# A planner that charges the time in which VectorE and GpSimd both work on SBUF, with three engines for one normalisation and a new table of terms

## The chip, the cores and the metric

The kernel runs on 1 core of one Trainium2 chip. The metric is the device time of one execution in microseconds, as the median of several runs. PE is TensorE, ACT ScalarE, DVE VectorE, POOL GpSimd, SP the queue that issues the DMAs.

## The reference

Three layers follow each other on 4 batches of 576 tokens and 512 features, all in fp32:

```
scores = scale * q @ k.T, within a window of 64 tokens     # 8 heads of 64
x = softmax(scores) @ v
h = relu(x @ w_in); u, v = halves of h                     # 512 -> 1024
v_n = (v - mean) / sqrt(var + 1e-6)
x = (u * (w_spatial @ v_n + b_spatial)) @ w_out
logits = x @ w_gate                                        # 4 experts, the best 2
for e in experts: ye = causal_softmax(scale*q_e @ k_e.T) @ v_e @ wo[e]
out = sum of the chosen experts' ye, weighted
```

## The kernel before

Precise products are made from two fp32r halves: a value is copied (the high half, names ending in `h`) and the copy is subtracted from it (the low half, `l`), and a product is three matmuls, as in `mm<-xh,w` and `mm<-xl,w`. So each tensor costs DVE, ACT or POOL a copy and a subtraction before PE can use it.

Phase 1 holds the first attention, the layer with `w_in` and the spatial mix; phase 2 holds the experts. In the first attention a **couple** (`a_couple`) is two groups of 192 tokens: 12 score matmuls `sc<-ut,qa` or `sc<-kt,qa`, then for each of two tiles `pa` the masked maximum on DVE (L501, three instructions each with a read of the accumulator), the exponential on ACT (L507, three), an addition and a reciprocal on DVE (L520, L522), the normalisation `s_norm` (L512, three, on POOL or DVE), three transposes on PE (L516, `at<-ident,pa`) and a copy to `pt`. Then 12 matmuls `at<-pt,v` (for the first batch `at<-pt,woh` and `at<-pt,wol`, tiles that hold `v` there) give `xh`, `xl`, which the projections `mm<-w,xh`, `mm<-xh,w` and so on read. `w_in` arrives as 64-bit words; `prep64` makes the two halves of it in six steps (L626 to L636, a copy, a subtraction). `b_mix` is the spatial mix; its first matmul is the first `mm<-wsp_h,vh`.

Nothing is issued in the order of the code. Each step is a node with its engines and their costs, and `Planner.run` walks through a modelled time: each engine takes the ready node of the lowest priority number, to which the table SHIFT adds a term for each unit of work; with several engines to choose from, a node goes where it would end first, with biases. The result is a fixed order of instructions for each engine. PE's plan also has 8 warming matmuls and 60 fillers `mm<-ident` of the lowest priority, which the plan uses where PE has nothing else. All 68 are issued, whether PE has then to wait or not.

Of the kernel before, what the change touches and what calls it, by code (L numbers as in the profile page):

```python
# [58 lines left out]


class Slot:
    def __init__(self, ring):
        self.nth, ring.asked = ring.asked, ring.asked + 1
        self.ring, self.make, self.left, self.free_at, self.t = ring, ring.make, 0, None, None

    def __getitem__(self, key):
        return self.t[key]


class Node:  # L70
    __slots__ = ("on", "emit", "prio", "wait", "next", "ready", "alloc", "use", "end", "by", "late", "form", "nth")


class Planner:
# [2 lines left out]
    ISSUE, WAY, RATE, FLIGHT = 475.0, 650.0, 360.0, 8  # L80
# [1284 lines left out]
```

## Time and profile before

| | |
|---|---|
| median of 3 runs | 464.27 us (462.72 to 464.32) |
| the profiled execution | 462.36 us, of which the span is 460.6 us |
| PE busy | 444.6 us (97%), 3962 matmuls |
| ACT, DVE, POOL busy | 289.1, 296.2, 159.7 us |
| granted TensorE clock | 0.999 of full speed |
| DMA | 32.97 MB, mean 72 GB/s |

The span runs from the first to the last instruction. PE's busy time contains the fillers and time in which matmuls overlap, so it is an upper bound of what PE has to do.

### The profile page before, as it was taken

How to read it: one execution, taken by the hardware profiler on the slowest of the kernel's cores; microseconds unless marked ns; L12 is line 12 of the kernel's file. 1: busy time of each engine (PE TensorE's matmuls, PEld its weight loads, DVE VectorE, ACT ScalarE, POOL GpSimd, SP SyncE). 2: the span in 40 equal slices, each digit the busy share in tenths (PEclk: the TensorE clock that was granted, in tenths of full speed). 3: DMA queues.
4: the chain of work that ended last, by engine and by line, in shares of the span. 5: the costliest groups of instructions: out<-in, count | busy, mean ns of one | idle time of the engine just before them, and what ended most of it. 6: DMA issues, size and time to landing. Idle time of an engine off the chain costs nothing.

```text
span 460.6 us, 10987 instructions
## 1 busy us (share of the span) xinstructions
PE 444.6 (97%) x3962; PEld 396.5 (86%) x3962; DVE 296.2 (64%) x1227; ACT 289.1 (63%) x906; POOL 159.7 (35%) x246
## 2 busy tenths in 40 slices
PE   7988998999999999999999999999999999999996
PEld 6766878997799988999899999888988988998875
DVE  3999899556583459912205346987876778858930
ACT  3867894647583337612224436898887797877953
POOL 6689587333831037700541442231031111200100
PEclk9999999999999999999999999999999999999999
DMA  8995334224242131301101000000001001000124
GB/s 268 356 308 161 124 93 156 71 78 135 65 133 61 47 91 52 89 1 54 39 1 21 26 1 2 0 2 1 1 25 46 24 2 22 25 2 1 55 85 137
DMA packets 31624, 32.97 MB, mean 72 GB/s; under 512 B 1937, under 2 KB 25489, under 8 KB 31570
## 3 DMA queue, kind: packets, MB, share of 16 engines
q1 hardware_dynamic: 31570, 32.28, 22.4%
q8 instruction: 31, 0.51, 0.4%
q14 instruction: 23, 0.19, 0.1%
HBM read 27.55 MB, written 4.72 MB: 70 GB/s over the span
## 4 chain that ended last, share of the span: by engine, by line
PE 79%; DVE 7%; DMA 4%; ACT 4%; POOL 3%; issue 1%; SPq 1%; POOLq 0%; ACTq 0%
PE mm L295 56%; PE sc L295 8%; PE at L295 8%; PE at L1180 4%; DMA y<-in_w_in_dram 3%; PE at L516 3%; ACT kd L306 1%; DVE pa L512 1%; POOL pa L512 1%; ACT p L1160 1%; SPq L384 1%; DVE wsp_l L319 1%; DVE xl L319 1%; ACT pg L306 1%; DMA qa<-in_qT_dram 1%
## 5 line engine op out<-in xcount | busy, mean ns | idle before, releaser
L295 PE MATMUL mm<-xh,w 128*128 128x288 f32 x512 | 110.3, 299 | 0.0
L295 PEld LDWEIGHTS mm<-xh,w 128*128 128x128 f32 x512 | 84.3, 188 | 1.2 <-issue 0.9
L295 PE MATMUL mm<-xl,w 128*128 128x288 f32 x256 | 75.4, 294 | 0.0
L295 PE MATMUL mm<-w,xh 128*128 128x512 f32 (+1 forms) x256 | 64.7, 342 | 0.0
L507 ACT ACTIVATE pa<-pa,mx 128x128 f32<-128x128 f32 x144 | 56.0, 395 | 9.7 <-DVE mx L501 9.5
L512 POOL TENSOR_SCALAR pa<-pa,mx 128x128 f32<-128x128 f32 x78 | 34.4, 456 | 54.5 <-ACT pa L507 29.6
L1164 POOL TENSOR_SCALAR p<-p,mc,fx 128x256 f32<-128x256 f32 (+4 forms) x24 | 16.0, 667 | 102.9 <-DVE mc L1163 48.4
L295 PEld LDWEIGHTS mm<-xl,w 128*128 128x128 f32 x256 | 48.2, 188 | 0.2
L295 PEld LDWEIGHTS mm<-w,xh 128*128 128x128 f32 x256 | 43.3, 189 | 5.0 <-issue 0.2
L1160 ACT ACTIVATE p<-p,mc 128x128 f32<-128x128 f32 (+4 forms) x72 | 41.9, 583 | 8.7 <-DVE mc L1148 4.4
L295 PE MATMUL mm<-w,xl 128*128 128x512 f32 (+1 forms) x128 | 43.2, 338 | 0.0
L295 PE MATMUL mm<-wsp_h,vh 128*128 128x288 f32 x128 | 39.0, 305 | 1.6 <-ACT ut L314 1.6
L295 PE MATMUL mm<-wsp_h,vl 128*128 128x288 f32 x128 | 37.7, 295 | 0.0
L295 PE MATMUL mm<-wsp_l,vh 128*128 128x288 f32 x128 | 37.7, 294 | 0.0
L1148 DVE CUSTOM_DVE_ANT_0 p<-sc,cmask 128x128 f32<-128x128 f32 (+4 forms) x72 | 33.7, 482 | 4.8 <-PE sc L295 3.1
L306 ACT ACTIVATE pg<-at 128x512 f32<-128x512 f32 (+4 forms) x80 | 32.3, 432 | 3.9 <-PE at L1180 3.2
L295 PE MATMUL sc<-kd,qs 128*64 128x288 f32 (+5 forms) x96 | 31.5, 342 | 0.1
L1180 PE MATMUL at<-ident,p 128*128 128x128 f32 x192 | 30.3, 276 | 1.0 <-DVE p L1164 0.3
L775 DVE TENSOR_TENSOR y<-mm,ut 128x288 f32<-128x288 f32 x24 | 10.8, 455 | 30.5 <-PE mm L295 30.5
L706 DVE BATCH_NORM_STATS2 st<-vr 128x6 f32<-128x512 f32 (+1 forms) x20 | 13.8, 690 | 25.8 <-ACT vr L314 25.4
L306 ACT ACTIVATE pt<-at 128x384 f32<-128x384 f32 x47 | 21.2, 490 | 14.0 <-PE at L516 14.0
L516 PE MATMUL at<-ident,pa 128*128 128x128 f32 x144 | 24.5, 285 | 5.7 <-DVE pa L512 3.3
(192 smaller groups left out, 1116.2 us busy)
## 6 DMA issues: line engine op xcount, KB each, us to landing
vt<-in_v_dram SPq DMA_DIRECT2D x12, 512.0 KB, 4.2
qa<-in_qT_dram SPq DMA_DIRECT2D x44, 96.0 KB, 3.2
out_dram<-ot SPq DMA_DIRECT2D x15, 256.0 KB, 2.0
y<-in_w_in_dram SPq DMA_DIRECT2D x7, 512.0 KB, 7.0
kt<-in_kT_dram SPq DMA_DIRECT2D x12, 288.0 KB, 3.1
y<-in_w_outT_dram SPq DMA_DIRECT2D x4, 512.0 KB, 3.4
y<-in_wspT_dram SPq DMA_DIRECT2D x2, 576.0 KB, 4.9
ut<-in_kT_dram SPq DMA_DIRECT2D x2, 384.0 KB, 7.5
```

The costliest lines, as they stand in the source:

```text
L295: pe.matmul(o, lhsT, rhs, start=start, stop=stop)
L306: act.activation(o, i, AF.Copy)
L319: engs[e].tensor_tensor(out=o, in0=a, in1=hi.bitcast(F32), op=ALU.subtract)
L507: act.activation(pa[:, j, :], pa[:, j, :], AF.Exp, bias=mx[:, j, 0:1], scale=-1.0, accum_out=mx[:, j, 1:2])
L512: engs[e].tensor_scalar(pa[:, j, :], pa[:, j, :], mx[:, j, 2:3], 1.0, op0=ALU.mult, op1=ALU.mult)
L516: pe.transpose(ps2[:, j * 128:(j + 1) * 128], pa[:, j, :], ident)
L706: a = N((DVE, 600), lambda e: dve.bn_stats(st[:m, 0:6], vr[:m]), [a], alloc=[st], use=[vr])
L775: dve.tensor_tensor(out=o, in0=ps[:, :HS], in1=u[:, d, tk], op=ALU.mult)
L1148: dve.tensor_tensor_reduce(out=P[:, a0:a1], in0=ps[:, :w], in1=msk, scale=-0.125, scalar=3.0e38, op0=ALU.add, op1=ALU.min, accum_out=mc[:, ...
L1160: a = N((ACT, 284 + 0.87 * L), lambda e: act.activation(P[:m, :L], P[:m, :L], AF.Exp, bias=mc[:m, 0:1], scale=-1.0, accum_out=mc[:m, 2:3]) ...
L1164: a = N({POOL: 328 + 0.832 * L, DVE: 90 + 0.52 * L}, lambda e: engs[e].tensor_scalar(P[:, :L], P[:, :L], mc[:, 3:4], fx[:, I, ev:ev + 1], ...
L1180: pe.transpose(ps[:, j * m:(j + 1) * m], P[:, j * 128:(j + 1) * 128], ident)
```

## The change

The planner's rules change in four places. A node says whether it works on SBUF alone (`sbuf=True`), and where such a node of DVE overlaps with an instruction of POOL, the plan adds the overlap to the one that starts later. A load that is issued while an earlier one is still on its way is charged 2.2 us more. The costs of switching PE between tile shapes, of score and PV groups and of matmuls change a little. And the normalisation of the first attention, `down` (the first step of `prep64`) and several copies out of PSUM may go to more engines than before. All scalars and the whole table SHIFT (3 rows of 351 terms, not shown) are replaced. The number of loads, matmuls and of all the other steps stays as it was.

```diff
-SWITCH = 58767.74293990493
+SWITCH = 227452.0
-DVE_BIAS = (1730.5970176011094, 7352.217706873879)
-POOL_BIAS = (288.01246154132895, 9897.664225472437)
+DVE_BIAS = (1146.0, 3886.0)
+POOL_BIAS = (1188.0, 5162.0)
-EFT = (772.5181606546909, 4334.303370577451)
+EFT = (534.0, 1231.0)
...
-    DRAIN = (0.0, 92.0, 91.0), (160.0, 0.0, 160.0), (75.0, 92.0, 0.0)
+    DRAIN = (0.0, 91.0, 91.0), (0.0, -78.0, 0.0), (0.0, 0.0, -78.0)
+
+    CLASH, BEHIND = 1.0, 2200.0
...
+        elif e == DVE:
+            if n.sbuf:
+                self.free[e] = n.end = n.end + self.CLASH * max(0.0, min(n.on[e], self.free[POOL] - t))
+            self.sbuf = n.sbuf
+        elif e == POOL and self.sbuf:
+            self.free[e] = n.end = n.end + self.CLASH * max(0.0, min(n.on[e], self.free[DVE] - t))
...
+                behind = self.BEHIND if self.moved[-1] > t + self.WAY else 0.0
...
-            self.free[e], n.end = t, self.moved[-1]
+            self.free[e], n.end = t, self.moved[-1] + behind
...
             def s_norm(e, pa=pa, mx=mx):
                 for j in range(3):
-                    engs[e].tensor_scalar(pa[:, j, :], pa[:, j, :], mx[:, j, 2:3], 1.0, op0=ALU.mult, op1=ALU.mult)
+                    if e == ACT:
+                        act.activation(pa[:, j, :], pa[:, j, :], AF.Copy, scale=mx[:, j, 2:3])
+                    else:
+                        engs[e].tensor_scalar(pa[:, j, :], pa[:, j, :], mx[:, j, 2:3], 1.0, op0=ALU.mult, op1=ALU.mult)
...
-            a = N({POOL: 1053, DVE: 450}, s_norm, [a], use=[pa, mx], prio=prio)
+            a = N({POOL: 1053, DVE: 450, ACT: 620}, s_norm, [a], use=[pa, mx], prio=prio, sbuf=True)
...
-        n1 = N((ACT, 520), lambda e: act.activation(a_(), word(1).bitcast(F32), AF.Copy, scale=2.0 ** -112),
-               [n0], alloc=[tmp], use=[raw], prio=prio)
...
+        n1 = N({ACT: 540, POOL: 620, DVE: 345}, down, [n0], alloc=[tmp], use=[raw], prio=prio, sbuf=True)
```

In the built program the normalisation's 144 instructions stand 78 on POOL and 66 on DVE before, and 114 on ACT, 24 on DVE and 6 on POOL in the change. POOL's rows shrink from 174 to 94.

The order moves at the start above all. First SP, the first loads, before and in the change (`ut` holds kT of the first batch, `qa` q, `woh` and `wol` v, `y` and `w` w_in):

```order
L384 DMA qa<-in_qT_dram 128x384 x2
L384 DMA y_128<-in_w_in_dram 128x1024
L384 DMA y_130<-in_w_in_dram 128x1024
L384 DMA ut<-in_kT_dram 128x2x192 x2
L384 DMA ut<-in_kT_dram 128x4x192
L384 DMA y_135<-in_w_in_dram 128x1024
```

```order
L394 DMA ut<-in_kT_dram 128x2x192 x2
L394 DMA qa<-in_qT_dram 128x384 x2
L394 DMA ut<-in_kT_dram 128x4x192
L394 DMA woh<-in_v_dram 128x2x256
L394 DMA wol<-in_v_dram 128x2x256
L394 DMA y_133<-in_w_in_dram 128x1024
```

kT is now ahead of q, and two loads of w_in that stood between q and kT come after v.

Then ACT, from its second shown instruction on, before and in the change (L507 and L517 are the exponential, L523 the normalisation, L630 and L645 `down`):

```order
L630 ACTIVATE y_140<-y_128 128x512
L630 ACTIVATE y_153<-y_130 128x512
L306 ACTIVATE w<-y_140 128x512
L507 ACTIVATE pa,mx<-pa,mx 128x128 x3
L630 ACTIVATE y_212<-y_135 128x512
L507 ACTIVATE pa,mx<-pa,mx 128x128 x3
L630 ACTIVATE w_252<-w_142 128x512
L507 ACTIVATE pa,mx<-pa,mx 128x128 x6
L306 ACTIVATE pt<-at 128x384
```

```order
L517 ACTIVATE pa,mx<-pa,mx 128x128 x6
L645 ACTIVATE y_226<-y_133 128x512
L316 ACTIVATE pt<-at 128x384
L517 ACTIVATE pa,mx<-pa,mx 128x128 x12
L523 ACTIVATE pa<-pa,mx 128x128 x3
L316 ACTIVATE w<-y_226 128x512
L316 ACTIVATE xh<-at 128x192 x2
L523 ACTIVATE pa<-pa,mx 128x128 x6
L316 ACTIVATE pt<-at 128x384 x3
```

ACT now begins with exponentials, and normalisations stand in its queue behind them.

Last PE, the rows around the last filler (`mm<-ident`) and the first projection (`mm<-w,xh`) in the change; before, the first projection stands behind five couples' scores, and 14 fillers stand behind it:

```order
L305 MATMUL mm<-ident 128x128 x7
L529 MATMUL at<-ident,pa 128x128 x3
L305 MATMUL mm<-ident 128x128 x10
L305 MATMUL sc<-ut,qa 64x128 x12
L305 MATMUL mm<-ident 128x128
L529 MATMUL at<-ident,pa 128x128 x6
L305 MATMUL sc<-kt,qa 64x128 x12
L305 MATMUL mm<-w,xh 128x512 x2
```

In the change seven couples' scores and all 68 warming matmuls and fillers stand ahead of the first projection.

## Rows read from the trace of the kernel before

**Rows 1.** Windows by stage: busy us (x instructions) of each engine.
```profile
0.00:9.81 9.81, 6.40 (x37) 6.24 (x37) 3.11 (x10) 2.67 (x4) 6.13 (x24) 1.00 0.76 248
9.81:78.15 68.34, 61.00 (x726) 50.14 (x726) 64.56 (x265) 51.40 (x188) 51.95 (x71) 1.00 0.66 211
78.15:250.00 171.85, 171.34 (x1674) 156.29 (x1675) 86.75 (x394) 82.30 (x288) 63.99 (x105) 1.00 0.21 62
250.00:450.00 200.00, 198.96 (x1495) 178.34 (x1494) 141.75 (x560) 149.17 (x422) 37.62 (x47) 1.00 0.06 20
450.00:460.60 10.60, 6.86 (x36) 5.48 (x34) 0.00 (x0) 3.62 (x7) 0.00 (x0) 0.97 0.45 148
```
Columns: stretch and its length, then busy time of PE, PEld, DVE, ACT, POOL, the granted clock, the DMA engines' busy share and GB/s.

**Rows 2.** Lines of PE from 0 to 80 us: busy us, mean ns | idle before.
```profile
L295 PE MATMUL mm<-ident 128*128 128x128 f32 x136 | 19.9, 301 | 1.6 <-DVE ident L325 1.6
```

**Rows 3.** Timeline of PE at the start: start us, length us, what [idle before <-releaser].
```profile
1.57 6.40 PE L295 MATMUL mm<-ident 128*128 128x128 f32 x36 [1.57 <-DVE ident L325]
9.81 0.89 PE L295 MATMUL sc<-ut,qa 64*64 64x128 f32 x24 [1.84 <-DMA ut<-in_kT_dram]
```

**Rows 4.** Timeline of PE where the spatial mix begins.
```profile
78.15 0.40 PE L295 MATMUL mm<-wsp_h,vh 128*128 128x288 f32 x1 [1.55 <-ACT ut L314]
```

**Rows 5.** The chain that ended last, 0 to 90 us: start us, us, what.
```profile
50.15 1.55 PE at L295 x48
...
83.72 0.66 PE at L516 x6
84.37 1.58 PE mm L295 x12
85.96 0.82 PE sc L295 x24
```

**Rows 6.** Lines of DVE from 0 to 80 us.
```profile
L501 DVE CUSTOM_DVE_ANT_0 pa<-sc,mask 128x128 f32<-128x128 f32 x54 | 12.6, 281 | 0.2 <-PE sc L295 0.2
L512 DVE TENSOR_SCALAR pa<-pa,mx 128x128 f32<-128x128 f32 x30 | 10.5, 408 | 0.1
L633 DVE SCALAR_TENSOR_TENSOR y<-y,y 128x512 int32<-128x512 int32 x10 | 8.1, 821 | 6.3 <-POOL y L626 6.2
L636 DVE SCALAR_TENSOR_TENSOR y<-y 128x512 int32<-128x512 int32 x10 | 7.7, 774 | 0.1
...
L319 DVE TENSOR_TENSOR wsp_l<-y,wsp_h 128x576 fp32r<-128x576 f32 x2 | 3.9, 1968 | 0.0
...
L628 DVE TENSOR_SCALAR y<-y 128x512 int32<-128x512 int32 x1 | 0.4, 398 | 0.0
```

**Rows 7.** Timelines of DVE and POOL, two normalisations on DVE.
```profile
13.21 2.41 DVE L512 TENSOR_SCALAR pa<-pa,mx 128x128 f32<-128x128 f32 x3
...
20.43 0.73 DVE L512 TENSOR_SCALAR pa<-pa,mx 128x128 f32<-128x128 f32 x3
21.08 0.70 DVE L636 SCALAR_TENSOR_TENSOR w<-w 128x512 int32<-128x512 int32 x1
...
13.03 1.27 POOL L319 TENSOR_TENSOR w<-y,w 128x512 fp32r<-128x512 f32 x1
14.26 0.65 POOL L626 TENSOR_SCALAR y<-y 128x512 f32<-128x512 f32 x1
```

**Rows 8.** Lines of ACT from 0 to 80 us, and its timeline at 282.8 us.
```profile
L507 ACT ACTIVATE pa<-pa,mx 128x128 f32<-128x128 f32 x60 | 23.3, 395 | 5.3 <-DVE mx L501 5.2
...
L630 ACT ACTIVATE y<-y 128x512 f32<-128x512 f32 x10 | 6.8, 678 | 7.3 <-DMA y<-in_w_in_dram 6.9 <-DVE t2w L319 0.4
...
282.80 0.91 ACT L306 ACTIVATE zt<-y 128x128 fp32r<-128x128 f32 x4
```

**Rows 9.** Windows of the first 20 us (columns as in rows 1).
```profile
0.00:10.00 10.00, 6.59 (x44) 6.43 (x48) 3.27 (x11) 2.86 (x4) 6.13 (x24) 1.00 0.77 251
10.00:20.00 10.00, 9.34 (x124) 8.01 (x120) 9.73 (x46) 8.20 (x34) 5.53 (x8) 1.00 1.05 366
```

**Rows 10.** Waits: engine line waited for: us in total, times, longest us.
```profile
ACT pa L507 <- DVE mx L501: 9.5, 10, 2.6
```

More of the change, by code (lines that the diff above doesn't have):

```diff
@@ L70 @@
 class Node:
-    __slots__ = ("on", "emit", "prio", "wait", "next", "ready", "alloc", "use", "end", "by", "late", "form", "nth")
+    __slots__ = ("on", "emit", "prio", "wait", "next", "ready", "alloc", "use", "end", "by", "late", "form", "nth", "sbuf")
 class Planner:
@@ L87, in __init__, with node @@
         self.phase = self.form = self.asked = 0
-    def node(self, on, emit, deps=(), alloc=(), use=(), prio=None, late=None, form=0):
+        self.sbuf = False
+    def node(self, on, emit, deps=(), alloc=(), use=(), prio=None, late=None, form=0, sbuf=False):
         n = Node()
-        n.form, n.nth = form, self.asked
+        n.form, n.nth, n.sbuf = form, self.asked, sbuf
         self.asked += 1
@@ L273, in t_mm @@
     def t_mm(n, m=128):
-        return max(109 if m == 128 else 53, 0.442 * n + 4.7)
+        return max(109 if m == 128 else 53, 0.4445 * n + 5.0)
     def t_act(n, psum_src=True):
@@ L545, in a_couple @@
         prio -= X_BIAS
-        o = N((PE, 760), pv, done + [PV_N.get(k[:2]) for k in grp] + vn, alloc=[ps3] + new, use=pts + hv, prio=prio,
+        o = N((PE, 848), pv, done + [PV_N.get(k[:2]) for k in grp] + vn, alloc=[ps3] + new, use=pts + hv, prio=prio,
               form=2)
@@ L554, in a_couple @@
                 cs, ss = slice(g * 192, g * 192 + w), slice(x * 192, x * 192 + w)
-                a = N((ACT, t_act(w)), lambda e, xh=xh, cs=cs, ss=ss: copy(e, xh[:, cs], ps3[:, ss]), [o], use=[ps3, xh], prio=prio)
+                a = N(on_copy(w), lambda e, xh=xh, cs=cs, ss=ss: copy(e, xh[:, cs], ps3[:, ss]), [o], use=[ps3, xh], prio=prio)
                 a = N((DVE, t_tt(w)), lambda e, xh=xh, xl=xl, cs=cs, ss=ss: sub(e, xl[:, cs], ps3[:, ss], xh[:, cs]), [a],
@@ L560, in a_couple @@
                 xt, ss = XT[b, p], slice(x * 192 + 128, x * 192 + 192)
-                a = N((ACT, 104), lambda e, xt=xt, ss=ss: copy(e, xt[:, 0, :], ps3[:, ss]), [o], use=[ps3, xt], prio=prio)
+                a = N(on_copy(64), lambda e, xt=xt, ss=ss: copy(e, xt[:, 0, :], ps3[:, ss]), [o], use=[ps3, xt], prio=prio)
                 XT_N[b, p] = N((DVE, 135), lambda e, xt=xt, ss=ss: sub(e, xt[:, 1, :], ps3[:, ss], xt[:, 0, :]), [a],
@@ L628, in sign, with down @@
                 dve.tensor_single_scalar(p_().bitcast(I32), word(1), SIGN, op=ALU.bitwise_and)
-        n1 = N((ACT, 520), lambda e: act.activation(a_(), word(1).bitcast(F32), AF.Copy, scale=2.0 ** -112),
-               [n0], alloc=[tmp], use=[raw], prio=prio)
-        n2 = N({POOL: 588, DVE: 335}, sign, [n0, n1], use=[raw, tmp], prio=prio)
+        def down(e):
+            if e == ACT:
+                act.activation(a_(), word(1).bitcast(F32), AF.Copy, scale=2.0 ** -112)
+            else:
+                engs[e].tensor_scalar(a_(), word(1).bitcast(F32), 2.0 ** -112, 1.0, op0=ALU.mult, op1=ALU.mult)
+        n1 = N({ACT: 540, POOL: 620, DVE: 345}, down, [n0], alloc=[tmp], use=[raw], prio=prio, sbuf=True)
+        n2 = N({POOL: 588, DVE: 335}, sign, [n0, n1], use=[raw, tmp], prio=prio, sbuf=True)
         n3 = N((DVE, 602), lambda e: dve.scalar_tensor_tensor(p_().bitcast(I32), word(0), 29, p_().bitcast(I32),
                                                               op0=ALU.logical_shift_right, op1=ALU.bitwise_or),
-               [n2], use=[raw, tmp], prio=prio)
+               [n2], use=[raw, tmp], prio=prio, sbuf=True)
         n4 = N((DVE, 602), lambda e: dve.scalar_tensor_tensor(a_().bitcast(I32), a_().bitcast(I32), 3, p_().bitcast(I32),
                                                               op0=ALU.logical_shift_left, op1=ALU.bitwise_or),
-               [n1, n3], use=[tmp], prio=prio)
+               [n1, n3], use=[tmp], prio=prio, sbuf=True)
         n5 = N(on_copy(512, 1, False), lambda e: copy(e, hv(), a_()), [n4, first],
-               alloc=alloc, use=[tmp] + ([] if alloc else [h]), prio=prio)
+               alloc=alloc, use=[tmp] + ([] if alloc else [h]), prio=prio, sbuf=True)
         if first is None:
             P_N[kind, k if kind == "in" else 0] = n5
-        return N({POOL: 1225, DVE: 602}, lambda e: sub(e, lv(), a_(), hv()), [n5], use=[tmp, h, l], prio=prio)
+        return N({POOL: 1225, DVE: 602}, lambda e: sub(e, lv(), a_(), hv()), [n5], use=[tmp, h, l], prio=prio, sbuf=True)
     def prep_sp(k0_, prio):
@@ L703, in b_v @@
             a = N((DVE, t_tt(512)), lambda e: dve.tensor_tensor(out=vr[:64], in0=ps[:64], in1=vr[:64], op=ALU.add), [a], use=[ps, vr])
-            a = N({ACT: 520, DVE: 335}, lambda e: relu(e, vr[:64], vr[:64]), [a], use=[vr])
+            a = N({ACT: 520, DVE: 335}, lambda e: relu(e, vr[:64], vr[:64]), [a], use=[vr], sbuf=True)
         a = N((DVE, 600), lambda e: dve.bn_stats(st[:m, 0:6], vr[:m]), [a], alloc=[st], use=[vr])
@@ L712, in b_v @@
         a = N({DVE: 460, POOL: 850}, lambda e: engs[e].tensor_scalar(
-            vr[:m], vr[:m], st[:m, 10:11], st[:m, 9:10], op0=ALU.add, op1=ALU.mult), [a, n2], use=[vr, st])
+            vr[:m], vr[:m], st[:m, 10:11], st[:m, 9:10], op0=ALU.add, op1=ALU.mult), [a, n2], use=[vr, st], sbuf=True)
         if t < 4:
@@ L716, in b_v @@
             VN[b, t] = vh, vl
-            a = N(on_copy(512, 1, False), lambda e: copy(e, vh.t, vr.t), [a], alloc=[vh], use=[vr])
-            a = N({POOL: 1225, DVE: 602}, lambda e: sub(e, vl.t, vr.t, vh.t), [a], alloc=[vl], use=[vr, vh])
+            a = N(on_copy(512, 1, False), lambda e: copy(e, vh.t, vr.t), [a], alloc=[vh], use=[vr], sbuf=True)
+            a = N({POOL: 1225, DVE: 602}, lambda e: sub(e, vl.t, vr.t, vh.t), [a], alloc=[vl], use=[vr, vh], sbuf=True)
         else:
@@ L724, in hi @@
                 copy(e, t2v[0:64], vr[:64])
-            a = N(on_copy(512, 2, False), hi, [a] + old, use=[vr])
-            a = N({DVE: 602}, lambda e: sub(e, t1v[64:128], vr[:64], t1v[0:64]), [a], use=[vr])
+            a = N(on_copy(512, 2, False), hi, [a] + old, use=[vr], sbuf=True)
+            a = N({DVE: 602}, lambda e: sub(e, t1v[64:128], vr[:64], t1v[0:64]), [a], use=[vr], sbuf=True)
         TAIL.setdefault(b, []).append(a)
@@ L787, in b_mix @@
             a = N(on_copy(HS, 1, False), lambda e: copy(e, yh[:, tk], gv(g)), [a] + ([] if new else YN[b, d]),
-                  alloc=new, use=[g] + ([] if new else [yh]))
+                  alloc=new, use=[g] + ([] if new else [yh]), sbuf=True)
             a = N({POOL: t_pool(HS), DVE: t_tt(HS)}, lambda e: sub(e, yl[:, tk], gv(g), yh[:, tk]), [a],
-                  use=[g, yh, yl])
+                  use=[g, yh, yl], sbuf=True)
         YN.setdefault((b, d), []).append(a)
@@ L822, in prep_w2 @@
             n1 = N(on_copy(w, 1, False), lambda e, sv=sv, ks=ks: copy(e, view(h.t)[:, ks], sv()),
-                   [n0] + ns, alloc=[h, l] if first else [], use=[st] + ([] if first else [h, l]), prio=prio + 3000)
+                   [n0] + ns, alloc=[h, l] if first else [], use=[st] + ([] if first else [h, l]), prio=prio + 3000, sbuf=True)
             n2 = N({POOL: t_pool(w), DVE: t_tt(w)}, lambda e, sv=sv, ks=ks: sub(e, view(l.t)[:, ks], sv(), view(h.t)[:, ks]),
-                   [n1], use=[st, h, l], prio=prio + 3000)
+                   [n1], use=[st, h, l], prio=prio + 3000, sbuf=True)
             ns.append(n2)
@@ L842, in fold @@
         FOLD.setdefault(nm, [a])
-        a = N((ACT, t_act(n)), lambda e: copy(e, view(oh.t)[:, i, :], ps[:, :n]), [a], use=[ps, oh, ol])
+        a = N(on_copy(n), lambda e: copy(e, view(oh.t)[:, i, :], ps[:, :n]), [a], use=[ps, oh, ol])
         a = N((DVE, t_tt(n)), lambda e: sub(e, view(ol.t)[:, i, :], ps[:, :n], view(oh.t)[:, i, :]), [a], use=[ps, oh, ol])
@@ L920, in go @@
                 engs[e].memset(ap, 0.0)
-        Z_N[key] = [N({POOL: c * len(aps), DVE: c * len(aps)}, go)]
+        Z_N[key] = [N({POOL: c * len(aps), DVE: c * len(aps)}, go, sbuf=True)]
     def zeros(pr):
@@ L952, in c_split @@
         h, l = YS[b, c] = r_xh.new(), r_xl.new()
-        a = N(on_copy(S, 1, False), lambda e: copy(e, h.t, y[:, c % 2, :]), YN[PH[b], c], alloc=[h], use=[y])
-        a = N({POOL: t_pool(S), DVE: t_tt(S)}, lambda e: sub(e, l.t, y[:, c % 2, :], h.t), [a], alloc=[l], use=[y, h])
+        a = N(on_copy(S, 1, False), lambda e: copy(e, h.t, y[:, c % 2, :]), YN[PH[b], c], alloc=[h], use=[y], sbuf=True)
+        a = N({POOL: t_pool(S), DVE: t_tt(S)}, lambda e: sub(e, l.t, y[:, c % 2, :], h.t), [a], alloc=[l], use=[y, h], sbuf=True)
         ZN[b, c] = [a]
@@ L1043, in c_vt @@
                     a = N(on_copy(64, 1, False), lambda e, x=x, c=c, h=h: copy(e, zh[:, c, x, :], h[:, 512:576]),
-                          ZN[0, c] + ns[:1], alloc=new, use=[h] + ([] if new else z))
+                          ZN[0, c] + ns[:1], alloc=new, use=[h] + ([] if new else z), sbuf=True)
                     a = N(on_copy(64, 1, False), lambda e, x=x, c=c, l=l: copy(e, zl[:, c, x, :], l[:, 512:576]),
-                          [a], use=[l] + z)
+                          [a], use=[l] + z, sbuf=True)
                 else:
@@ L1050, in c_vt @@
                     a = N(on_copy(128, 1, False), lambda e, x=x, cc=cc, y=y: copy(e, zh[:, cc, x, :], y[:, :, 512:576]),
-                          YN[PH[b + x], c] + YN[PH[b + x], c + 1] + ns[:1], alloc=new, use=[y] + ([] if new else z))
+                          YN[PH[b + x], c] + YN[PH[b + x], c + 1] + ns[:1], alloc=new, use=[y] + ([] if new else z), sbuf=True)
                     a = N({POOL: t_pool(128), DVE: t_tt(128)}, lambda e, x=x, cc=cc, y=y: sub(
-                        e, zl[:, cc, x, :], y[:, :, 512:576], zh[:, cc, x, :]), [a], use=[y] + z)
+                        e, zl[:, cc, x, :], y[:, :, 512:576], zh[:, cc, x, :]), [a], use=[y] + z, sbuf=True)
                 ns.append(a)
@@ L1151, in unit @@
             zn = [n for x in both for n in Z_N["k", pr, x]]
-            a = N((PE, 2 * len(both) * t_mm(a1 - a0, m)), s_mm, QK_N[b, pr, "q"] + QK_N[b, pr, "k"] + zn, alloc=[ps],
+            a = N((PE, 80 + 2 * len(both) * t_mm(a1 - a0, m)), s_mm, QK_N[b, pr, "q"] + QK_N[b, pr, "k"] + zn, alloc=[ps],
                   use=[x[y] for x in (qs, kd, kl) for y in both], prio=prio)
@@ L1165, in unit @@
             P[:, :L], P[:, :L], mc[:, 3:4], fx[:, I, ev:ev + 1], op0=ALU.mult, op1=ALU.mult), [a, fn],
-              use=[P, mc, fx], prio=prio)
+              use=[P, mc, fx], prio=prio, sbuf=True)
         grp = 0 if I < 2 else 1
@@ L1187, in unit @@
         f, an = a, PG_N[key][:1]
-        a = N((PE, nj * 109), tr, [f] + an, alloc=[ps] + ([pg] if first else []), use=[P], prio=prio)
+        a = N((PE, nj * 109 - 40), tr, [f] + an, alloc=[ps] + ([pg] if first else []), use=[P], prio=prio)
         if first:
@@ L1225, in c_pv @@
         cs = slice(i0, i0 + 256)
-        o = N((PE, 780 if grp == 0 else 2200), go, PG_N[b, pr, grp] + V2_N[b] + (VT_N[b] if grp else []) + ([] if new else O_N[b, pr][:1]),
+        o = N((PE, 800 if grp == 0 else 2200), go, PG_N[b, pr, grp] + V2_N[b] + (VT_N[b] if grp else []) + ([] if new else O_N[b, pr][:1]),
               alloc=[ps] + new, use=[pg, v2] + ([vt] if grp else []), prio=prio, form=2)
-        a = N((ACT, t_act(256)), lambda e: copy(e, oh[:, cs], ps[:, :256]), [o], use=[ps, oh], prio=prio)
+        a = N(on_copy(256), lambda e: copy(e, oh[:, cs], ps[:, :256]), [o], use=[ps, oh], prio=prio)
         a = N((DVE, t_tt(256)), lambda e: sub(e, ol[:, cs], ps[:, :256], oh[:, cs]), [a], use=[ps, oh, ol], prio=prio)
```

14 lines of the change are left out of this document (7 added, 7 removed), and 6 rows, old and new, of the table SHIFT.

## The prediction

> **What bounds the kernel now.** I first cut the span into stages [rows 1]. From 78.15 us to 450 us PE is busy 370.3 of 371.9 us: nothing another engine does faster there can be worth more than 1.6 us, apart from gaps too short to count as idle. The last 10.6 us hold the last matmuls, the copy and the store, and the change issues the same rows there. So what can be won lies ahead of 78.15 us. That is where the spatial mix begins, with PE having waited 1.55 us for it [rows 4]. I take this matmul as the **marker**, since all of w_in, the spatial weights and five normalised tiles must be ready for it in both kernels.
>
> From the first score, at 9.81 us, which waited 1.84 us for kT [rows 3], to the marker are 68.3 us [rows 1]. DVE is busy 64.6 us of them (94%), POOL 52.0 (76%), ACT 51.4 (75%). PE shows 61.0 us, but part of it is no work: warming matmuls and fillers take 19.9 us by 80 us [rows 2], of which 6.4 us lie ahead of the first score [rows 3], so 13.5 us lie behind it. PE's real work in the stretch is at most 61.0 - 13.5 = 47.5 us: here PE follows DVE.
>
> DVE itself is slowed. Three normalisations on DVE took 2.41 us from 13.21, while POOL worked through a subtraction and the instruction behind it; at 20.43 the next instruction started 0.65 us after the same three [rows 7]. Over the start one costs 10.5/30 = 0.35 us, and a 576-column subtraction 1.97 us [rows 6].
>
> **The change part by part.** I compare what stands ahead of the marker in the two programs, from the order of instructions.
>
> *PE does more ahead of the marker.* Before: 10 score groups, 9 PV groups, 54 transposes and 116 projection matmuls. In the change: 13, 10, 63 and 152. The difference is 3 x 0.82 + 0.78 + 9 x 0.11 + 36 x 0.132 = 9.0 us [rows 5] (a group of scores 0.82; two PV groups 1.55; six transposes 0.66; twelve matmuls 1.58). All 68 warming matmuls and fillers stand ahead of the marker in both. PE's total work is the same, so if the marker came at the same time, the kernel would end 9.0 us earlier. The gain is 9.0 us minus the marker's delay.
>
> *The first loads.* Ahead of the first scores, q and two w_in chunks give way to kT. Before, PE's 18 first matmuls end at 7.97 us and the scores start at 9.81 [rows 3]. In the change 15 stand there, so PE is free near 7.0 us. By 5.6 MiB of loads the fourth w_in chunk of the first half has been asked for. The DMA engines moved 2.5 MB in the first 10 us and 3.7 MB in the next 10 [rows 9], so it lands near 20 to 21 us. Its six steps cost some 5 us in a row (0.65 to 1.27 us each [rows 6, 7, 8]). The first projection can't start before 1.6 us + 17 to 20 us of fillers [rows 2] + 11 us of work, near 30 us. That hides the later w_in by some 4 us; with that cover gone each us of lateness costs one. I take the first score at 7.0 us: 2.8 us won, between 0 (kT no earlier) and 2.8.
>
> *DVE.* The marker waits for 260 DVE instructions before and 290 in the change. Out go 18 normalisations (18 x 0.35 = 6.3 us), one 576-column subtraction (1.97) and two long instructions (some 2.4, between 0.8 and 3.9): 10.7 us. In come 12 masked maxima with their reads (12 x 12.6/54 = 2.8 us), 19 middle-sized copies and subtractions (by L628's 0.4 us, 7.6; 0.2 to 0.7 us each) and 8 small ones (some 1.3): 11.7 us [rows 6]. Net +1 us. Against it stands less contention: 20 L633/L636 took 0.80 us on the mean and 0.70 at 21.08 [rows 6, 7], 2 us in all, and more elsewhere; but POOL's work ahead of the marker only falls from some 40 to 35 us, so I take 3 us, between 0 and 6. DVE then needs 64.6 + 1 - 3 = 62.6 us, about as much as before.
>
> *ACT.* 129 instructions before, 170 in the change. In come 45 normalisations, 3 exponentials and 5 copies; out go 8 `down` steps and two long copies, and some short ones. No ACT normalisation is in this trace. The nearest row is ACT's 128x128 copy within SBUF: four took 0.91 us, so 0.20 each, the last one's tail aside [rows 8]. That makes 45 x 0.20 = 9.0, + 3 x 0.39, + 5 x 0.68, - 10 x 0.68, - 0.3 = +6.5 us, to 57.9 us. The bounds of the price are 0.20 and the 0.39 of an exponential of the same shape [rows 8].
>
> *The marker's new time.* If DVE keeps its 94%, the marker comes at 7.0 + 62.6/0.94 = 73.6 us: gain 9.0 + 4.5 = 13.5 us. If ACT can do no more than the 75% it did, 7.0 + 57.9/0.75 = 84.2: gain 3.0 us. Neither engine was ever the other's equal in this trace: now both are close, each waits for the other within a couple, and some of both shares will be lost. I choose the middle, 8 us: the marker near 79 us with DVE at 87% and ACT at 80%.
>
> *Behind the marker.* The other 23 sets of three normalisations on ACT add 69 x 0.20 = 13.8 us there, on 82.3 of 171.9 us; with further copies some 98 us in 164, 60%. POOL's normalisations in phase 2 go to DVE (17 more of some 0.5 us), 141.8 us become 150 of 200. PE hides both now: it was idle 0.5 and 1.0 us [rows 1]. Two busier engines will give it some more short waits; I take 1 us back, 0 to 3. PE's switches between tile shapes stay nearly as many (24 visits to score groups in both, 21 and 22 to PV), so the new switch costs change nothing on PE by themselves.
>
> Sum: -8 + 1 = -7 us; the profiled execution's 462.4 becomes 455.4, with the runs' median 1.9 us above it: 457. As the likelier errors (more contention gone) lie below, I say **456 us**.
>
> The Trainium skill speaks against the move: ScalarE: Activation LUTs, Rules for kernel authors, has multiplications done on VectorE and not on ScalarE, and budgets about 0.3 us for an ACTIVATE and 0.83 ns an element. That would be 0.41 us for one of these, an estimate from that page, and twice the 0.20 us that this trace shows for a copy of the shape; by it the sum would come out near no gain. That is nearly the third rival's price.
>
> **The rivals.**
> 1. *ACT takes DVE's place as the bound.* For it: the 75%, and exponentials that had to wait for DVE 0.95 us each time [rows 10]. Against: ACT had 17 us free there. The marker comes at 84 us or a little later, and with 1 us lost behind it the gain is 0 to 2 us: 463 us.
> 2. *Normalisations block ACT's queue* (slower). A normalisation waits for DVE's reciprocal, and exponentials, PV copies and relus of the layer stand behind it. A wait on DVE costs ACT 0.95 us on the mean [rows 10]; there are 38 sets. From 0.3 us of it on PE in each (11 us) the gain is gone and the kernel is slower: 468 us. Against: PE has had other work behind the marker.
> 3. *An ACT normalisation costs 0.39 us, not 0.20.* Then ACT needs 66.5 us ahead of the marker; at 80% that is 90 us, 12 us later than before, 3 us more than the 9.0, and with the 1 us the time is 468 us. The four copies in [rows 8] speak against it.
> 4. *Contention was nearly all of it.* DVE needs 59.6 us, at 94% to 70.4 us: gain 16.7 us, 448 us. PE's own work and fillers end there near 70 us, so no more can be won.
>
> **How the numbers follow.** Chances: forecast (gain 3 to 13.5 us at the marker) 0.62, rival 1 0.14, rival 2 0.10, rival 3 0.04, rival 4 0.10. The likeliest case's own range is 450 to 462. For 8 in 10 I leave out the slower rivals and the far end of the fourth: 447 to 464 us. Half a per cent, 2.3 us, is about what a measurement can tell from no change. Faster by more: the forecast nearly whole and rival 4, 0.71. Within it: rival 1 and an edge of the forecast, 0.15. Slower: rivals 2 and 3, 0.14.
>
> **What would show it.** In the changed kernel's profile: the first score near 7 us, with no wait for kT; the marker between 73 and 84 us; DVE's and ACT's busy shares ahead of it 85 to 90% and about 80%; ACT's normalisations at 0.20 us from start to start; DVE's normalisations back to 0.2 us; POOL's busy time near 70 us; PE idle no more than 3 us from the marker to 450 us. The prediction is wrong if ACT's idle time is put down to DVE's reciprocals, if the first projection waits for w_in well past 30 us, or if PE shows new waits in phase 2, where DVE is fuller.

## The result and the profile after

| | before | after |
|---|---|---|
| time, us: median (lowest to highest, 4 runs each) | 464.29 (462.72 to 465.20) | 456.17 (455.76 to 456.80) |
| profiled execution: time, span | 462.4, 460.6 | 456.8, 455.0 |
| first score / marker / first `sc<-kd` | 9.81 / 78.15 / 291.56 | 7.14 / 79.55 / 281.66 |

The ratio is 0.983 with a 95% interval of 0.980 to 0.986: faster by 8.1 us, for 456.0 predicted. The profiled execution of before lies near the low end of its runs and that of the changed kernel is the slowest of its four, so the two spans differ by 5.6 us only, and all that follows on where the time went is told of the spans. PE's granted clock has a part in the runs' spread: the four executions of the changed kernel had 0.998 to 1.000 of full speed, and of 48 executions of before that were timed beside the experiments, the 22 with 0.998 or more have a median of 463.4 us, the 10 with less than 0.994 one of 464.5.

The windows of the changed kernel answer to [rows 1]. Columns: stretch, its length, then busy time of PE, PEld, DVE, ACT, POOL, the granted clock, the DMA engines' busy share, GB/s.
```profile
0.00:7.14 7.14, 5.34 (x30) 5.23 (x30) 1.91 (x8) 1.28 (x1) 4.70 (x22) 1.00 0.67 186
7.14:79.55 72.41, 69.33 (x874) 59.00 (x873) 65.84 (x285) 66.50 (x252) 35.58 (x41) 1.00 0.70 220
79.55:250.00 170.45, 170.45 (x1613) 157.33 (x1610) 98.24 (x391) 99.83 (x334) 19.85 (x27) 1.00 0.22 63
250.00:445.00 195.00, 190.93 (x1421) 168.85 (x1420) 143.87 (x582) 148.62 (x418) 11.06 (x15) 1.00 0.05 17
```
In the second row DVE is busy 91% of the stretch ahead of the marker and ACT 92%; before it was 94% and 75%. In the third PE has no gap. The fourth is the bad one: 4.1 us idle, for 1.0 us in the 200 us of [rows 1].

The timeline of PE, at the first score, the marker and the start of the second phase; it answers to [rows 3, 4].
```profile
1.79 5.42 PE L305 MATMUL mm<-ident 128*128 128x128 f32 x30 [1.79 <-DVE ident L335]
7.14 0.89 PE L305 MATMUL sc<-ut,qa 64*64 64x128 f32 x24
...
79.55 0.40 PE L305 MATMUL mm<-wsp_h,vh 128*128 128x288 f32 x1
...
281.66 0.22 PE L305 MATMUL sc<-kd,qs 128*128 128x128 f32 x1
```
Neither the first score nor the marker has a wait behind it any more. From the first `sc<-kd` both kernels have the second phase ahead of them: 460.59 - 291.56 = 169.0 us before, 455.03 - 281.66 = 173.4 us after. So the first phase became 9.9 us shorter and the second 4.3 us longer. Of the 9.9 us, 9.0 - 1.4 = 7.6 are there at the marker, if PE does 9.0 us more ahead of it as the forecast estimated; 2.3 more come behind it. The two traces bear the estimate out: from the marker to the second phase PE took 213.4 us before and 202.1 after, and counted by kind of matmul, with each kind's time from start to start, 9.2 of these 11.3 us are matmuls that no longer stand there. The other 2.1 are matmuls that follow each other faster, 1.1 of it at the transposes (0.097 us each for 0.111).

The lines of ACT and DVE from 0 to 79.55 us, which answer to [rows 6, 8], and ACT's timeline at one set of normalisations.
```profile
L517 ACT ACTIVATE pa<-pa,mx 128x128 f32<-128x128 f32 x69 | 26.8, 398 | 9.1 <-DVE mx L511 9.0
L523 ACT ACTIVATE pa<-pa,mx 128x128 f32<-128x128 f32 x48 | 15.3, 396 | 1.2 <-DVE mx L535 0.9
...
L651 DVE SCALAR_TENSOR_TENSOR y<-y,y 128x512 int32<-128x512 int32 x9 | 7.0, 775 | 0.0
L654 DVE SCALAR_TENSOR_TENSOR y<-y 128x512 int32<-128x512 int32 x8 | 5.3, 668 | 0.0
L525 DVE TENSOR_SCALAR pa<-pa,mx 128x128 f32<-128x128 f32 x12 | 4.7, 450 | 0.1
...
17.82 0.99 ACT L523 ACTIVATE pa<-pa,mx 128x128 f32<-128x128 f32 x3
18.71 0.61 ACT L316 ACTIVATE w<-y 128x512 fp32r<-128x512 f32 x1
```
L523 is the normalisation on ACT. Three of them start at 17.82 and the next instruction at 18.71: 0.30 us each, not the 0.20 of the copies of [rows 8]. ACT waits for a reciprocal (L535) only 0.9 us in all.

PE's waits from 250 us on: for whom, us in total, times, longest.
```profile
PE sc L305 <- DVE mc L1166: 1.8, 3, 0.9
PE at L1198 <- DVE p L1182: 1.6, 3, 0.7
```
Both are waits for DVE in the second phase; L1182 is the second attention's normalisation. The kernel before has nothing of the first and, of the second, only this:
```profile
PE at L1180 <- DVE p L1164: 0.3, 1, 0.3
```

### The profile page after: what moved, and what is told of

Read it like the earlier page. It is cut to its first block, busy times and chain, and to the rows that moved or that the text cites. A ratio compares the mean times of both kernels' runs of the same rounds, so it can differ in the third digit from the quotient of the medians.

```text
span 455.0 us, 10875 instructions
## 1 busy us (share of the span) xinstructions
PE 442.3 (97%) x3962; PEld 395.4 (87%) x3962; DVE 309.9 (68%) x1264; ACT 319.3 (70%) x1010; POOL 71.2 (16%) x105
## 4 chain that ended last, share of the span: by engine, by line
PE 68%; ACT 15%; DVE 13%; issue 2%; POOL 0%; ACTq 0%; POOLq 0%; DVEq 0%
PE mm L305 51%; PE at L305 6%; PE sc L305 6%; PE at L1198 3%; ACT p L1178 3%; ACT kd L316 3%; ACT pa L517 2%; DVE p L1166 2%; PE at L529 2%; DVE qs L329 2%; ACT pa L523 2%; DVE pa L511 1%; ACT pt L316 1%; DVE p L1182 1%; ACT xh L316 1%
## 5 line engine op out<-in xcount | busy, mean ns | idle before, releaser
L517 ACT ACTIVATE pa<-pa,mx 128x128 f32<-128x128 f32 x144 | 56.0, 398 | 13.8 <-DVE mx L511 13.8
L523 ACT ACTIVATE pa<-pa,mx 128x128 f32<-128x128 f32 x114 | 36.7, 395 | 4.3 <-DVE mx L535 3.6
L316 ACT ACTIVATE pg<-at 128x128 f32<-128x128 f32 (+4 forms) x80 | 32.7, 432 | 3.0 <-PE at L1198 2.1
L305 PE MATMUL sc<-kd,qs 128*128 128x128 f32 (+5 forms) x96 | 32.5, 348 | 2.0 <-DVE mc L1166 1.8
L511 DVE CUSTOM_DVE_ANT_0 pa<-sc,mask 128x128 f32<-128x128 f32 x120 | 28.2, 284 | 7.4 <-PE sc L305 5.3
L728 POOL TENSOR_TENSOR st<-st,nhalf 128x1 f32<-128x1 f32 (+1 forms) x20 | 12.0, 598 | 130.2 <-DVE st L727 130.2
L1182 POOL TENSOR_SCALAR p<-p,mc,fx 128x512 f32<-128x512 f32 (+2 forms) x7 | 6.3, 903 | 159.4 <-PE at L1198 50.7
L1182 DVE TENSOR_SCALAR p<-p,mc,fx 128x128 f32<-128x128 f32 (+4 forms) x65 | 29.1, 452 | 1.4
L305 PE MATMUL sc<-kz,qs 128*128 128x128 f32 (+5 forms) x96 | 29.1, 313 | 0.0
```

What stands on the lines that cost most here:

```text
L305: pe.matmul(o, lhsT, rhs, start=start, stop=stop)
L316: act.activation(o, i, AF.Copy)
L511: dve.tensor_tensor_reduce(out=pa[:, j, :], in0=ps[:, j * 128:(j + 1) * 128], in1=mask(j), scale=-0.125, scalar=3.0e38, op0=ALU.add, op1=A ...
L517: act.activation(pa[:, j, :], pa[:, j, :], AF.Exp, bias=mx[:, j, 0:1], scale=-1.0, accum_out=mx[:, j, 1:2])
L523: act.activation(pa[:, j, :], pa[:, j, :], AF.Copy, scale=mx[:, j, 2:3])
L728: a = N((POOL, 464), lambda e: pool.tensor_tensor(out=st[:m, 9:10], in0=st[:m, 8:9], in1=nhalf[:m], op=ALU.pow), [n1], use=[st])
```

## The experiments

**The two phases apart.** The planner plans the first phase (up to the last projection) and the second one by one, so one kernel can have the new plan for one and the old plan for the other. All numbers, rules and stage costs became pairs, and table units up to 170 belong to the first phase. The first kernel, cut:
```diff
-SWITCH = 227452.0
-DVE_BIAS = (1146.0, 3886.0)
-POOL_BIAS = (1188.0, 5162.0)
-EFT = (534.0, 1231.0)
+SWITCH = (227452.0, 58767.74293990493)
+DVE_BIAS = (1146.0, 7352.217706873879)
+POOL_BIAS = (1188.0, 9897.664225472437)
+EFT = (534.0, 4334.303370577451)
+NEW = (True, False)
...
-    CLASH, BEHIND = 1.0, 2200.0
+    CLASH, BEHIND = [1.0 if x else 0.0 for x in NEW], [2200.0 if x else 0.0 for x in NEW]
```


> The first phase planned as in the changed kernel, the second as in the kernel before (its table rows, biases, stage costs and rules; nearly its old order there). Theory: the change gained about 10 us in the first phase and gave about 4.3 us back in the second, so this one gives nothing back: about 452 us, PE's first sc<-kd as early as in the changed kernel and PE idle under 1.5 us from 250 us to 445 us (changed kernel: some 4 us). Rival: the second phase lost only because it began 10 us earlier, with other work (splits, folded weights, loads) not yet ready: then this one loses the same 4 us and stays near 456 us.

> The mirror image: first phase as in the kernel before, second phase as in the changed one. Theory: the marker and the end of the first phase stand as before and the second phase costs some 4 us more: about 468 us. Rival (the second phase's plan is as good as the old one, and only the earlier start hurt it): 464 us.

Measured, with ratios to the kernel before timed beside each: 452.76 us (0.977, 0.9755 to 0.9787), faster than both kernels; and 467.70 us (1.009, 1.0076 to 1.0103) for the mirror image, which has `NEW = (False, True)`. The first one's window, to be held against the fourth row above:
```profile
250.00:445.00 195.00, 193.98 (x1444) 172.70 (x1443) 138.43 (x552) 149.86 (x422) 33.07 (x44) 1.00 0.06 21
```
PE idles 1.0 us for 4.1. From the first `sc<-kd` to the end the old plan takes 169.3 us here, and 173.3 us pass with the new plan behind the old first phase. The earlier start does the second phase no harm; its new plan does. In the profiles of all twelve experiments and of the two kernels, the second phase takes 169.0 to 169.5 us wherever its old plan is unedited (five kernels) and 173.3 to 173.7 with the new one (seven), whenever it begins. PE's order in it is the same in each of the two sets.

Is it the engine? The old plan has 24 normalisations of the second attention and 7 splits of x on POOL, the new one 7 and none. Two kernels move them and leave each engine's other instructions in place.
```diff
-        a = N({POOL: 328 + 0.832 * L, DVE: 90 + 0.52 * L}, lambda e: engs[e].tensor_scalar(
+        a = N({POOL: 328 + 0.832 * L, DVE: 90 + 0.52 * L}, lambda e: dve.tensor_scalar(
...
-        a = N({POOL: t_pool(S), DVE: t_tt(S)}, lambda e: sub(e, l.t, y[:, c % 2, :], h.t), [a], alloc=[l], use=[y, h], sbuf=True)
+        a = N({POOL: t_pool(S), DVE: t_tt(S)}, lambda e: sub(DVE, l.t, y[:, c % 2, :], h.t), [a], alloc=[l], use=[y, h], sbuf=True)
```
The other puts the old plan's 24 on POOL (a set, of which four members are shown) and all the rest on DVE:
```diff
+ON_POOL = {(0, 0, 0, 1), (0, 0, 0, 4), (0, 0, 1, 0), (0, 0, 1, 1),
...
-        a = N({POOL: 328 + 0.832 * L, DVE: 90 + 0.52 * L}, lambda e: engs[e].tensor_scalar(
+        a = N({POOL: 328 + 0.832 * L, DVE: 90 + 0.52 * L}, lambda e: engs[POOL if (b, pr, ev % 2, I) in ON_POOL else DVE].tensor_scalar(
```


> As the first run, with the second phase's normalisations and splits that stand on POOL (24 and 7) put on DVE, every engine's order else the same. Theory of the second phase's loss A: DVE, which in the changed kernel took 17 normalisations and 7 splits over from POOL, became late for PE: then this costs 2 to 4 us against the first run (454 to 456 us). Theory B: the order of the new plan lost the time, not the engine: then within 1 us of the first run, since DVE has 30 us of 200 idle or more there.

> The changed kernel with the 24 normalisations of the second phase put on POOL that stood there in the run with the old second phase (7 others that stood on POOL go to DVE), all else in its place. If DVE's taking them over is half of the second phase's loss, as the 1.7 us of the run on DVE alone say: 454 to 455 us. If the new order of PE has its places where POOL's longer normalisation comes too late: 456 us or more.

Measured: 454.44 us (0.9811, 0.9793 to 0.983), so 1.7 us lost by the move to DVE, a little under the 2 to 4 us expected; its profile shows 1.7 us of PE's waits for the normalisation in 6 places, with the second phase at 171.1 us. The reverse move in the changed kernel didn't win this back: 459.32 us (0.9899, 0.988 to 0.9918), 3.1 us slower than it was, the second phase at 175.4 us; PE now waits for POOL:
```profile
PE at L1199 <- POOL p L1183: 1.5, 4, 0.7
PE sc L306 <- DVE mc L1167: 1.0, 2, 0.6
```
Either engine loses in the other's plan. That a normalisation's place in the order and its engine belong together is the reading that fits both; neither move alone accounts for the 4.3 us.

**The normalisation's engine in the first phase, order unchanged.** The kernel before with POOL's 78 normalisations issued on ACT, and the changed kernel with ACT's 114 issued on DVE.
```diff
                 for j in range(3):
-                    engs[e].tensor_scalar(pa[:, j, :], pa[:, j, :], mx[:, j, 2:3], 1.0, op0=ALU.mult, op1=ALU.mult)
+                    if e == POOL:
+                        act.activation(pa[:, j, :], pa[:, j, :], AF.Copy, scale=mx[:, j, 2:3])
+                    else:
+                        engs[e].tensor_scalar(pa[:, j, :], pa[:, j, :], mx[:, j, 2:3], 1.0, op0=ALU.mult, op1=ALU.mult)
```
```diff
-                    if e == ACT:
-                        act.activation(pa[:, j, :], pa[:, j, :], AF.Copy, scale=mx[:, j, 2:3])
-                    else:
-                        engs[e].tensor_scalar(pa[:, j, :], pa[:, j, :], mx[:, j, 2:3], 1.0, op0=ALU.mult, op1=ALU.mult)
+                    engs[DVE if e == ACT else e].tensor_scalar(pa[:, j, :], pa[:, j, :], mx[:, j, 2:3], 1.0, op0=ALU.mult, op1=ALU.mult)
```


> The kernel before with the 78 normalisations of the first attention that stood on POOL put on ACT, every other instruction in its old place. Theory of the prediction (DVE's sum sets the marker, and POOL's work beside it makes it longer): POOL loses 16.5 us ahead of the marker, DVE's sum there falls by some 3 us from 64.6 us, ACT's rises from 51.4 to some 58 us; marker near 75 us, time 460 to 462 us. Rival 1 (order alone gains, the move nothing): marker 78, 464 us. Rival 2 (ACT's queue held up by the normalisations): marker over 79, 466 us or more.

Measured: 470.14 us (1.015, 1.0132 to 1.0168), the marker at 82.34. There is some relief, but it is small. The same 275 DVE instructions stand ahead of the marker in both kernels, and kept DVE busy for 67.7 us before and 66.6 here (up to the marker, before and then here):
```profile
0.00:78.15 78.15, 67.40 (x762) 56.38 (x762) 67.67 (x275) 54.07 (x191) 58.08 (x95) 1.00 0.67 216
0.00:82.34 82.34, 70.62 (x762) 60.19 (x762) 66.62 (x275) 61.56 (x221) 44.66 (x66) 0.96 0.66 205
```
The spatial weights' subtraction halved against [rows 6], while DVE's 30 normalisations stayed at 0.41 us on the mean:
```profile
L319 DVE TENSOR_TENSOR wsp_l<-y,wsp_h 128x576 fp32r<-128x576 f32 x2 | 1.9, 926 | 0.0
```
And the kernel was slower. The chain that ended last, just ahead of the marker (start us, us, what), shows by whom:
```profile
73.45 0.19 DVE mx L525
73.82 0.21 issue
74.03 0.68 ACT pa L513 x2
74.73 0.41 ACT ut L314
75.15 0.22 ACT xh L306
75.37 0.52 ACT vr L314
75.91 0.69 DVE st L709
77.09 0.69 DVE y L636
77.85 3.51 DMA y<-in_w_outT_dram
81.50 0.40 issue
81.90 0.40 ACT ut L314
82.34 1.73 PE mm L295 x11
```
ACT's timeline has the wait, 3.52 us:
```profile
73.72 0.99 ACT L513 ACTIVATE pa<-pa,mx 128x128 f32<-128x128 f32 x3 [3.52 <-DVE mx L525]
```
ACT stands at a normalisation (L513) until DVE's reciprocal (L525) is there; relu and copies queue behind it, DVE's steps behind those, a buffer comes free late and its load lands late. This is the second rival's blocking. It need not be the whole loss of 7.4 us up to the second phase, which begins at 298.95 us for 291.56: PE's granted clock fell to 0.66 from 10 to 15 us and from 75 to 80 us, which is 2 x 5 x 0.34 = 3.4 us of PE's time at the most.

> The changed kernel with its 114 ACT normalisations put on DVE, all else in its place. Ahead of the marker 48 of them come to DVE, at 0.2 us each without and 0.4 us with POOL at work beside them: 10 to 19 us on DVE's 67.8 us. Theory (ACT's share is what lets the marker come at 79.6 us with 9 us more of PE's work ahead of it): marker 88 to 95 us, time 464 to 470 us. Rival (DVE had room, the new order of PE and of the loads gained): marker within 2 us of 79.6, time 456 to 458 us.

Measured: 465.15 us (1.0034, 1.0018 to 1.005): 9.0 us lost, the whole gain and a little more. The marker comes at 85.98 us, 6.4 late and somewhat less than expected. Its windows from 30 to 50 us:
```profile
30.00:40.00 10.00, 6.66 (x70) 4.88 (x69) 9.06 (x42) 5.95 (x23) 3.88 (x4) 0.82 0.60 190
40.00:50.00 10.00, 10.00 (x103) 8.07 (x103) 9.41 (x45) 5.94 (x24) 4.11 (x5) 0.84 0.45 117
```
DVE is nine tenths busy, ACT six, and PE idles 3.3 us. The changed order needs ACT's share. The clock fell here too: by 0.18 and 0.16 in these two windows, 3.4 us of PE's time at the most, so at least 3.0 of the 6.4 us are not the clock.

**One part alone in the kernel before.** The planner of before may choose ACT too (the branch that then issues the step on ACT, as in the change, is not shown); and, apart from that, the first two loads of kT go out ahead of two of qT and two of w_in (`HOLD` is 6).
```diff
-            a = N({POOL: 1053, DVE: 450}, s_norm, [a], use=[pa, mx], prio=prio)
+            a = N({POOL: 1053, DVE: 450, ACT: 620}, s_norm, [a], use=[pa, mx], prio=prio)
```
```diff
-        n.emit(e)
+        if e == SP and len(self.held) < HOLD:
+            self.held.append(n.emit)
+            for f in self.held[-2:] + self.held[:-2] if len(self.held) == HOLD else []:
+                f(e)
+        else:
+            n.emit(e)
```


> The kernel before with one thing of the change: its planner may put a normalisation of the first attention on ACT as well (60 of 144 go there, 72 stay on POOL, 12 on DVE; 49 rows of PE's order differ), with the old numbers and rules. If the third engine alone gains: DVE is freed of 54 normalisations, marker 74 to 76 us, time 460 to 462 us. If, as with the moved POOL normalisations, an order that was fitted to other engines loses more than the relief gives: 464 to 470 us.

> The kernel before with the two first loads of kT issued ahead of the two of qT and two of w_in, nothing else moved. Prediction's term: first score at 7 instead of 9.8 us, 2.8 us that a start bound by DVE gives on in full: marker 75 to 76 us, time 461 to 462 us. Rival: the loads of w_in that come later hold the start back, and the marker stays at 78: 464 us.

Measured: 462.26 us with ACT allowed (0.9976, 0.9958 to 0.9994), a gain of 1.2 us, short of what the third engine alone was to gain but no loss either (its profiled execution, at 464.62 us the slowest of its ten, does not tell where); and 464.84 us with kT first (1.0016, 1.0005 to 1.0027), no gain, the marker at 80.35. Its timelines of ACT and DVE at the start say where the early score went, and under them that of DVE in the kernel before:
```profile
8.85 0.68 ACT L637 ACTIVATE y<-y 128x512 f32<-128x512 f32 x1 [6.83 <-DMA y<-in_w_in_dram]
9.66 0.69 DVE L640 SCALAR_TENSOR_TENSOR y<-y,y 128x512 int32<-128x512 int32 x1 [6.69 <-POOL y L633]
11.70 0.69 DVE L640 SCALAR_TENSOR_TENSOR y<-y,y 128x512 int32<-128x512 int32 x1 [0.54 <-POOL y L633]
12.30 0.28 DVE L508 CUSTOM_DVE_ANT_0 pa<-sc,mask 128x128 f32<-128x128 f32 x1
```
```profile
7.66 0.69 DVE L633 SCALAR_TENSOR_TENSOR y<-y,y 128x512 int32<-128x512 int32 x1 [4.69 <-POOL y L626]
9.84 0.69 DVE L633 SCALAR_TENSOR_TENSOR y<-y,y 128x512 int32<-128x512 int32 x1 [0.69 <-POOL y L626]
10.73 0.29 DVE L501 CUSTOM_DVE_ANT_0 pa<-sc,mask 128x128 f32<-128x128 f32 x1 [0.20 <-PE sc L295]
```
The first score starts at 7.49 us instead of 9.81, but the first masked maximum of it at 12.30 instead of 10.73: three steps on w_in stand ahead of it in DVE's queue, and they begin 2.0 us later because w_in lands later. The granted clock fell as well, to 0.54 from 15 to 20 us and 0.78 from 20 to 25, so how much of the early score each of the two took is not separated. The changed kernel has the loads and DVE's queue turned round together: its first maximum starts at 8.08 us with no step on w_in ahead of it.

**Plans made anew.** Two kernels take one rule or choice from the changed kernel, and two controls move a number that means little.
```diff
-            a = N({POOL: 1053, DVE: 450, ACT: 620}, s_norm, [a], use=[pa, mx], prio=prio, sbuf=True)
+            a = N({POOL: 1053, DVE: 450}, s_norm, [a], use=[pa, mx], prio=prio, sbuf=True)
```
```diff
-    CLASH, BEHIND = 1.0, 2200.0
+    CLASH, BEHIND = 0.0, 2200.0
```
```diff
-EFT = (534.0, 1231.0)
+EFT = (560.0, 1231.0)
```
```diff
-            a = N({POOL: 1053, DVE: 450, ACT: 620}, s_norm, [a], use=[pa, mx], prio=prio, sbuf=True)
+            a = N({POOL: 1053, DVE: 450, ACT: 640}, s_norm, [a], use=[pa, mx], prio=prio, sbuf=True)
```


> The changed kernel with its planner barred from ACT for the first attention's normalisations (57 on POOL, 87 on DVE), its rules and numbers kept. If the third engine is what the gain rests on: DVE's sum ahead of the marker over 72 us, marker 84 us or later, time 461 to 466 us. If rules and numbers carry it: 456 to 458 us.

> The changed kernel planned without the charge for DVE and POOL at work together (the charge set to 0), the rest kept: 105 normalisations stay on ACT, 33 on DVE, 6 on POOL. If the charge carries part of the gain: DVE's instructions grow longer in the first 80 us and the time is 458 us or more. If the third engine took the normalisations off POOL anyway: within 1.5 us of 456.2.

> A control for the runs in which the plan was made anew: the changed kernel with a number that has no bearing on rules or engines off by 26 ns (EFT of the first phase 560 for 534), which moves 303 rows of PE's order. If the table of units is fitted to this very plan, the time is 465 to 475 us, as without the charge or without ACT; if those two runs lost by what they left out, this one stays within 3 us of 456.2.

> A second control: the price of ACT's normalisation 640 ns for 620 ns in the planner alone, which moves 248 rows of PE's order. Expected as for the first control: 465 to 475 us if the table is fitted to one plan, within 3 us of 456.2 if not.

Measured: 473.06 us without ACT, 473.51 without the charge, 475.60 with `EFT` at 560, 466.33 with the price at 640 (ratios 1.020, 1.019, 1.024 and 1.004). The first had been expected at 461 to 466 us at the worst. The loss is in the first phase each time: its end moves from 281.7 us to 298.0, 299.5, 300.8 and 290.0. A part of it can be PE's clock, which averaged 0.986, 0.988, 0.986 and 0.992 of full speed in these profiles and 1.000 in that of the changed kernel: (1 - 0.986) x 471.3 = 6.6 us at the most in the first, 3.7 in the last. The marker does not tell the loss: with the price at 640 it comes at 75.76 us, 3.8 us earlier than in the changed kernel, because less of PE's work stands ahead of it. A number off by 26 ns costs as much as a whole rule: the table of units suits this plan and none of the others tried, and the first two runs say nothing of what the rule or the choice is worth. That the charge itself helps is not shown by any run here.

## Why the prediction was right, and what in it was not

- **The marker: right, by sums that were not.** Forecast near 79 us with a gain of 8; measured 79.55 and 7.6. The 9.0 us of work that PE does more ahead of it were right (9.2 by the traces). But DVE had 65.8 us to do for the 62.6 said and ACT 66.5 for 57.9, and both were busy 91 to 92% for the 87 and 80% said. More work and fewer mutual waits cancelled, which is luck. That ACT's share is needed for it was shown from the other side (9.0 us lost when its normalisations went to DVE).
- **ACT's price: mis-sized.** The step took 0.20 us from a copy whose factor is fixed in the instruction. With a factor for each partition (`scale=mx`) it is 0.293 us from start to start (the median of 83 pairs), 45 x 0.093 = 4.2 us more ahead of the marker. The Trainium skill, ScalarE: Activation LUTs, What ACT_TABLE_LOAD costs, says that each such pointer operand adds some 93 ns; the two prices of this trace, 0.200 and 0.293, agree. The rest of ACT's 8.6 us is mostly work done ahead of need: 69 exponentials for 60 [rows 8], where the marker needed 3 more, (9 - 3) x 0.39 = 2.3 us, and 3 normalisations beyond the 45, 0.9.
- **The first loads: the cause fell.** The first score came at 7.14, as said, but "2.8 us won" is not a gain by itself: with DVE's old order it gave nothing. The first projection, said near 30 us, started at 35.1 us, and PE shows no wait for w_in there.
- **Contention: there, but mis-sized.** The forecast took 3 us of relief for DVE and had POOL's work ahead of the marker fall from some 40 to 35 us. By the windows it fell from 58.1 to 40.3 us; over the whole span POOL was busy 71 us, as forecast. Taking 30 of POOL's normalisations away, with the order as it was, relieved DVE by 1.1 us only, and the kernel grew slower. In the changed kernel the steps from which the forecast worked its relief out, L633 and L636 before and L651 and L654 now, took (7.0 + 5.3) / 17 = 0.72 us on the mean, for 0.80 before and 0.70 said; what the relief there is in all, no run shows, since the order differs too. It isn't gone there: DVE's normalisations took 284 ns in the median but 450 on the mean ahead of the marker, so "back to 0.2 us" (from start to start) was wrong for some.
- **Behind the marker: the mis-sized term.** Said: 1 us back, 0 to 3, and PE idle at most 3 us to 450 us. Measured: 2.3 us more gained up to the second phase, then 4.3 lost in it, net 2.0, and 4.1 us idle from 250 to 445 alone. That busier engines cost something was right, that PE "hides both now" was not: PE shows new waits for DVE in the second phase, which the forecast named as a sign of being wrong, and the loss is the second phase's new plan (452.76 us without it). The 2.3 us lie where PE shows no waits to speak of in either kernel, and where the forecast saw no more than 1.6 us to win, save in gaps too short to count as idle: PE's matmuls followed each other faster there. Why the transposes did was not tried.
- **The sum.** 7 us were forecast between the two profiled executions, 5.6 came (7.6 + 2.3 - 4.3). The medians differ by 8.1, which brought the forecast to within 0.2 us of the result. The two errors, 0.4 at the marker and 1.0 behind it, point the same way, and each is small only because larger ones inside it cancelled: more work against fewer waits, 2.3 us won against 4.3 lost. The last step, from 457 to 456 us for more contention gone, is not borne out, since both errors made the gain smaller; the distance of the medians made up for it. That the number was so close is luck, while the way it went and the rough size of the gain were reasoned.
- **The rivals.** The first in part: ACT has 15% of the chain that ended last, for 4% before, but the marker did not slip to 84. The second is real when the engine changes and the order does not (470.14). The third's 0.39 us was too high, the fourth's 448 us too low.

## What to carry to other kernels

Where engines run their queues in order, a cheaper engine for a step may pay only with an order that fits it: POOL's 78 normalisations moved to ACT in the old order cost 6.5 us here. Compare stretches between fixed matmuls, not only whole times, and count what stands ahead of each: the 8 us hid a phase that had become 4.3 us slower, and taking the old plan for it gave the best kernel, 452.76 us. Look at the granted clock of every run before a loss is put down to waits alone. And before a re-planned variant is read as evidence on a rule, run a control that disturbs the plan by as much.
